# A decode layer's weight stream in five 32 KB load slots instead of ten of 16 KB

## The chip, the cores and the metric

The kernel runs on one core of one Trainium2 chip. The metric is the device time of one execution in microseconds, and lower is better. Before the change the median of three runs is 140.44 us (140.40 to 140.49).

## The reference

The kernel computes one decoding step of a transformer layer for four sequences of one token each: attention over the last 2048 entries of a KV cache, then a gated feed-forward block. All inputs are bfloat16.

```python
# x (4,1,1024); k_cache, v_cache (4,4,8192,128); wq (1024,4096); wo (4096,1024)
# w1, w3 (1024,3584); w2 (3584,1024);  W = 2048, 32 query heads on 4 KV heads, Dh = 128
q = (layernorm(x) @ wq) per head
p = softmax(q @ k[last W].T * Dh**-0.5)
h = x + (p @ v[last W]) @ wo
n = layernorm(h)
out = h + (silu(n @ w1) * (n @ w3)) @ w2
```

Four rows of activations meet 55.6 MB of caches and weights, and each of those bytes is read once.

## The kernel before

**The stream.** Everything large passes through a pool of `NSLOT = 10` slots of `SLOT = 8192` bfloat16 elements per partition, that is 16 KB on each of 128 partitions, 2 MB in all. `ring` is the order written out by hand: the keys of the four sequences, then the pieces of `wq` interleaved with four entries `kT` that take a slot but load nothing (they hold transposed keys), then values, `wo`, `w1`, `w3` and `w2`. An entry of k, v, `wq` and `wo` is 2 MB, one contiguous run of 16 KB on each partition. `w1` and `w3` come in four entries each of two weight rows, 14 KB on each partition. `w2` comes in blocks of 8, 8, 8, 2 and 2 rows (`W2B`), a row being 2 KB per partition. That is 29 loads, all issued by SyncE (SP) at L118.

**When a load is issued.** `fill` (L110) walks through the ring as long as the entry ten places before has been marked by `done`; the tile pool then makes SP wait until the last reader of the slot has finished. SP takes its loads in order. Completion is counted on eight semaphores used in turn, so that a load also waits until the load eight before it (counting the four small loads of x on ScalarE's queue) has landed.

**The stages on TensorE**, in the order in which they are written:

1. Keys are transposed (L226) in blocks of eight and copied to `kT` by VectorE (L228) and ScalarE (L230) in turn.
2. The query projection (L244) consumes `wq` entry by entry, 16 matmuls for each.
3. For each sequence: `scores` (L279), `row_max`, `softmax` (L319), `transpose_p` (L331) and `output` (L354), staggered over the sequences by the loop at L375.
4. The output projection with `wo` (L419), the residual and the second layernorm (L429 to L203).
5. `up_projection` (L443) with `w1`, 16 matmuls for each entry; its exponential, reciprocal and product on ScalarE and VectorE (L457 to L461); then `up_projection` with `w3`, the product `hg` (L465) and its transpose `hg_T` (L210).
6. The down projection (L476) through `w2`, four matmuls per row, then the sum with `h1` (L486) and four small stores.

Of the kernel before, what the change touches and what calls it, by code (L numbers as in the profile page):

```python
# [10 lines left out]
P = 128  # L11
# [3 lines left out]
BF16 = mybir.dt.bfloat16  # L15
FP32 = mybir.dt.float32

NSLOT = 10
SLOT = 8192
NEG = -1.0e30  # L20


@with_exitstack
def kernel(
# [20 lines left out]
    nc = tc.nc  # L45

    B, _, D = A_x.shape
    Hkv, Sk, Dh = A_k_cache.shape[1], A_k_cache.shape[2], A_k_cache.shape[3]
    NQ = A_wq.shape[1]
# [3 lines left out]
    F = B_w1.shape[1]  # L53
    KC = D // P
# [14 lines left out]
    wq_v = A_wq.rearrange("(p kc) n -> p kc n", kc=KC)  # L69
    T = REP  # L70
    L5 = 8
    JR = W // R
    JB = 8
    JM = 4
    wo_v = A_wo.rearrange("(g p t) n -> p g (t n)", g=Hkv, t=T)
    w1_v = B_w1.rearrange("(p kc) f -> p kc f", kc=KC)
    w3_v = B_w3.rearrange("(p kc) f -> p kc f", kc=KC)
    w2_v = B_w2.rearrange("(p fc) n -> p fc n", fc=FC)
# [4 lines left out]
    ptpool = ctx.enter_context(tc.tile_pool(name="ptpool", bufs=3))  # L83
    stream = ctx.enter_context(tc.tile_pool(name="stream", bufs=NSLOT))
    ps = ctx.enter_context(tc.tile_pool(name="ps", bufs=1, space=bass.MemoryType.PSUM))
# [3 lines left out]
    def of_cache(cache, b):  # L89
        return cache[b, :, Sk - W : Sk, :].rearrange("g (i j) d -> i g (j d)", j=JR)  # L90

    ks = [("k", b, [JR, Dh], of_cache(A_k_cache, b)) for b in range(B)]
    vs = [("v", b, [JR, Dh], of_cache(A_v_cache, b)) for b in range(B)]
    kts = [("kT", b, [JR, P], None) for b in range(B)]
    wqs = [("wq", i, [2, NQ], wq_v[:, 2 * i : 2 * i + 2, :]) for i in range(KC // 2)]
    wos = [("wo", g, [1, T * D], wo_v[:, g : g + 1, :]) for g in range(Hkv)]
    ring = ks + [x for two in zip(kts, wqs) for x in two] + vs + wos
    for name, w_v in (("w1", w1_v), ("w3", w3_v)):
        for i in range(KC // 2):
            ring.append((name, i, [2, F], w_v[:, 2 * i : 2 * i + 2, :]))  # L100
    W2B = [8, 8, 8, 2, 2]
    f0 = 0
    for i, n in enumerate(W2B):
        ring.append(("w2", i, [n, D], w2_v[:, f0 : f0 + n, :]))
        f0 += n
    place = {(name, i): at for at, (name, i, _, _) in enumerate(ring)}
    views = []
    used = set()

    def fill():  # L110

        while len(views) < len(ring) and (len(views) < NSLOT or len(views) - NSLOT in used):
            name, i, shape, src = ring[len(views)]
            slot = stream.tile([P, SLOT], BF16, tag="slot", name="s_" + name)
            dst = slot[:, : int(np.prod(shape))]
            view = dst.rearrange("p (a b) -> p a b", a=shape[0])
            if src is not None:
                nc.sync.dma_start(out=dst if name in ("k", "v") else view, in_=src)  # L118
            views.append(view)

    def get(name, i):
        return views[place[(name, i)]]

    def done(name, i):
        used.add(place[(name, i)])
        fill()

    ctx.enter_context(tc.manual_schedule())
# [4 lines left out]
    for c in range(C):  # L133
        nc.scalar.dma_start(out=x_nat[R * c : R * c + B, :], in_=x_flat[:, c * DQ : (c + 1) * DQ])
    fill()

    ident = const.tile([P, P], BF16)
# [8 lines left out]
        out=t32[:], in_=ident[:].rearrange("p (q h) -> p h q", q=C), axis=AX.X, op=ALU.add  # L146
# [4 lines left out]
    for q in range(C):  # L151
# [3 lines left out]
        out=negm[:], in_=t32[:].rearrange("p (g r) -> p g r", g=Hkv), axis=AX.X, op=ALU.add  # L155
    )
    nc.vector.tensor_scalar(
        out=negm[:], in0=negm[:], scalar1=-1.0, scalar2=-NEG, op0=ALU.add, op1=ALU.mult
    )
    jmask = const.tile([P, JM, 1], FP32)  # L160
    nc.vector.tensor_reduce(
        out=jmask[:, :, 0], in_=ident[:].rearrange("p (j h) -> p j h", j=JM), axis=AX.X, op=ALU.add
# [6 lines left out]
    for l in range(2):  # L169
        nc.gpsimd.tensor_copy(  # L170
            out=strip[:, l, B - 1 :].rearrange("p (c x) -> p c x", c=C)[:, :, : B * Hkv].rearrange(
                "p c (g b) -> p c g b", b=B
            )[:, :, :, 0],
            in_=t32[:].rearrange("p (g c l) -> p l c g", g=Hkv, c=C)[:, l],
# [45 lines left out]
    for b in range(B):  # L220
        k = get("k", b)
        kT = get("kT", b)
        for jb in range(JR // JB):
            kt_ps = ps.tile([P, JB, P], BF16, tag=f"kt{n_step % 3}")
            for jj in range(JB):
                nc.tensor.transpose(out=kt_ps[:, jj], in_=k[:, jb * JB + jj, :], identity=ident[:])  # L226
            if n_step % 2 == 0:
                nc.vector.tensor_copy(out=kT[:, jb * JB : (jb + 1) * JB], in_=kt_ps[:])  # L228
            else:
                nc.scalar.copy(out=kT[:, jb * JB : (jb + 1) * JB], in_=kt_ps[:])  # L230
            n_step += 1
        done("k", b)
# [1 line left out]

    q_ps = [ps.tile([P, REP // 2, Dh], FP32, tag=f"sc{hf}", name=f"q_ps{hf}") for hf in range(2)]
    HALF = REP // 2
    for i in range(KC // 2):
        w = get("wq", i)
        for kk in range(2):
            kc = 2 * i + kk  # L240
            for hf in range(2):
                for c in range(C):
                    o = (2 * c + hf) * HALF * Dh
                    nc.tensor.matmul(  # L244
                        q_ps[hf][R * c : R * c + R],
                        lhsT=xn_T[:, kc, :],
                        rhs=w[:, kk, o : o + HALF * Dh],
                        start=(kc == 0),
                        stop=(kc == KC - 1),
                        tile_position=(0, R * c),  # L250
                    )
        done("wq", i)
# [10 lines left out]
    for b in range(B):  # L263
        nc.vector.tensor_copy(  # L264
            out=Qm[:, b].rearrange("p (g y) -> p g y", y=QW)[:, :, :REP],
            in_=qT_ps[:, :, :, b].rearrange("p r g -> p g r"),
# [8 lines left out]
    def scores(b, gs):  # L275
        v = get("kT", b).rearrange("p j (q i g) -> p g q j i", q=C, g=Hkv)
        for g in gs:
            for q in range(C):
                nc.tensor.matmul(  # L279
                    sc_ps[b][R * q : R * q + R],  # L280
                    lhsT=Qm[:, b, g * R : (g + 1) * R],
                    rhs=v[:, g, q],
                    start=(g == 0),
                    stop=(g == Hkv - 1),
                    tile_position=(0, R * q),
                )
        if Hkv - 1 in gs:
            done("kT", b)
# [103 lines left out]
    for l in range(2):  # L392
# [15 lines left out]
        out=oP[:, :, :, :B],  # L408
        in_=oX[:, :, : Hkv * B].rearrange("p t (g b) -> p g t b", b=B),
# [4 lines left out]
    for g in range(Hkv):  # L414
        w = get("wo", g)
        for t in range(T):
            for c in range(C):
                o = t * D + c * DQ
# [14 lines left out]


    def up_projection(name, out_ps):
        for i in range(KC // 2):
            w = get(name, i)
            for kk in range(2):
                kc = 2 * i + kk
                for hf in range(2):  # L440
                    for c in range(C):
                        o = c * FQ + hf * FH
                        nc.tensor.matmul(  # L443
                            out_ps[hf][R * c : R * c + R],
                            lhsT=hn_T[:, kc, :],
                            rhs=w[:, kk, o : o + FH],
                            start=(kc == 0),
                            stop=(kc == KC - 1),
                            tile_position=(0, R * c),
                        )  # L450
            done(name, i)

    gu_ps = [ps.tile([P, FH], FP32, tag=f"sc{i}", name=f"gu_ps{i}") for i in range(4)]
    up_projection("w1", gu_ps[:2])
    eg = act.tile([P, 2, FH], FP32)
    for hf in range(2):
# [3 lines left out]
    for hf in range(2):  # L460
        nc.vector.tensor_tensor(out=eg[:, hf], in0=gu_ps[hf][:], in1=eg[:, hf], op=ALU.mult)  # L461
    up_projection("w3", gu_ps[2:])
    hg = act.tile([P, 2, FH], BF16)
    for hf in range(2):
# [6 lines left out]
    fc = 0  # L471
    for i, n in enumerate(W2B):
        w = get("w2", i)
# [46 lines left out]
```

## Time and profile before

| | |
|---|---|
| median of 3 runs | 140.44 us |
| the profiled execution's own time | 140.35 us |
| its span, first to last instruction | 138.5 us |
| outside the span | 1.85 us |
| read from HBM | 55.58 MB, mean 401 GB/s over the span |
| TensorE matmul / VectorE / ScalarE / GpSimd busy | 76.9 / 52.5 / 43.2 / 4.2 us |
| mean granted TensorE clock | 0.787 of full speed |

The page gives busy time by engine, the span in 40 slices with the DMA engines' busy share and rate, the traffic of each DMA queue, and the chain of work that ended last. Besides the page, the answers of the trace used below are the table by stretches of time, the timeline of single engines, and the records of DMA packets. A packet record is one descriptor on one of the 16 DMA engines: its queue, size, start and duration; a packet of 4 bytes is the mark with which one engine reports that its part of a load has landed.

### The profile page before, as it was taken

Reading aid. Unit: us, or ns where it says so; the run is one execution under the profiler, and the core shown is the slowest. Engines: PE = TensorE matmul, PEld = TensorE weight load, DVE = VectorE, ACT = ScalarE, POOL = GpSimd, SP = SyncE. Lnnn points to the kernel's source line nnn. Section 1 sums busy time; section 2 is a strip of 40 time slices with the busy share of each in tenths; the row PEclk is TensorE's granted clock in tenths of the full one; section 3 lists DMA queues with packets and bytes.
Section 4 is the critical chain, followed back from the end, with each engine's and each line's share of the span. In section 5 each row is a group of like instructions: output and inputs, shape, how many; then the busy total and the mean of one; then the engine's idle time right before and its main releaser. Section 6 shows DMA issues by size and latency. Waiting matters only on the chain.

```text
span 138.5 us, 2042 instructions
## 1 busy us (share of the span) xinstructions
PE 76.9 (55%) x868; PEld 45.8 (33%) x868; DVE 52.5 (38%) x97; ACT 43.2 (31%) x57; POOL 4.2 (3%) x18
## 2 busy tenths in 40 slices
PE   0009999971153799059639979483632432352280
PEld 0009988851011332024223535372311110142150
DVE  3026566630000334457365595515249700610001
ACT  2103799970000508999419600000420000000000
POOL 7400000000000000000000000000000000000000
PEclk9999999999555559955995999999999555555555
DMA  4999999999999999999999999999999999999940
GB/s 147 403 432 445 426 416 440 421 421 435 426 421 440 421 428 426 416 435 435 416 435 433 416 440 410 435 414 435 418 431 426 426 427 431 421 435 431 390 182 2
DMA packets 4249, 55.72 MB, mean 402 GB/s; under 512 B 496, under 2 KB 528, under 8 KB 784
## 3 DMA queue, kind: packets, MB, share of 16 engines
q1 hardware_dynamic: 4192, 55.58, 94.8%
q8 instruction: 7, 0.11, 0.3%
q10 hardware_dynamic: 48, 0.01, 0.0%
q14 instruction: 2, 0.02, 0.0%
HBM read 55.58 MB, written 0.01 MB: 401 GB/s over the span
## 4 chain that ended last, share of the span: by engine, by line
DMA 68%; PE 18%; DVE 6%; ACT 4%; issue 1%; SPq 1%; DVEq 0%
DMA s_w<-in_B_w_dram 38%; DMA s_wq<-in_A_wq_dram 24%; PE o_ps L354 10%; DMA s_k<-in_A_k_cache_dram 6%; ACT P L319 4%; PE sc_ps L279 4%; DVE PT L331 2%; PE q_ps L244 1%; PE nm_ps L308 1%; SPq L118 1%; DVE rmax L293 1%; PE mx_ps L295 1%; PE qT_ps L258 1%; DVE om L371 1%; PE tot_ps L340 1%
## 5 line engine op out<-in xcount | busy, mean ns | idle before, releaser
L319 ACT ACTIVATE P<-sc_ps,bias 128x512 bf16<-128x512 f32 x16 | 19.7, 1420 | 9.9 <-DVE bias L316 9.9
L226 PE MATMUL kt_ps<-ident,s_k 128*128 128x128 bf16 x256 | 18.4, 232 | 0.3
L226 PEld LDWEIGHTS <-s_k 128*128 128x128 bf16 x256 | 16.8, 105 | 1.9 <-issue 1.2
L354 PE MATMUL o_ps<-s_v,PT 128*128 128x512 bf16 x64 | 17.5, 435 | 0.0
L230 ACT COPY s_kT<-kt_ps 128x1024 bf16<-128x1024 bf16 x16 | 16.2, 1012 | 2.2 <-PE kt_ps L226 1.3
L443 PE MATMUL gu_ps<-s_w,n_T 128*32 128x448 bf16 x128 | 9.2, 435 | 13.4 <-DMA s_w<-in_B_w_dram 11.6
L228 DVE COPY s_kT<-kt_ps 128x1024 bf16<-128x1024 bf16 x16 | 11.1, 691 | 6.0 <-PE kt_ps L226 6.0
L476 PE MATMUL y_ps<-s_w,hg_T 128*32 128x256 bf16 x112 | 6.7, 416 | 9.4 <-DMA s_w<-in_B_w_dram 9.4
L244 PE MATMUL q_ps<-s_wq,n_T 128*32 128x512 bf16 x64 | 5.9, 503 | 10.4 <-DMA s_wq<-in_A_wq_dram 10.4
L331 DVE STREAM_TRANSPOSE PT<-P 128x2048 bf16<-128x2048 bf16 x4 | 9.2, 2302 | 2.7 <-ACT P L319 2.7
L354 PEld LDWEIGHTS <-PT 128*128 128x128 bf16 x64 | 7.1, 116 | 8.9 <-issue 4.2
L443 PEld LDWEIGHTS <-n_T 128*32 128x32 bf16 x128 | 3.9, 109 | 18.0 <-issue 14.6
L279 PE MATMUL sc_ps<-s_kT,Qm 128*32 128x512 bf16 x64 | 8.8, 608 | 0.4 <-DVE Qm L264 0.4
L193 ACT ACTIVATE rstd<-rstd,eps_t 128x4 f32<-128x4 f32 x2 | 0.6, 298 | 26.7 <-DVE rstd L192 26.7
L476 PEld LDWEIGHTS <-hg_T 128*32 128x32 bf16 x112 | 4.7, 138 | 11.7 <-issue 7.6
L183 PE MATMUL sums_ps<-both,ones_f 128*128 128x64 f32 x4 | 1.1, 374 | 11.9 <-DVE both L181 11.9
L254 DVE CAST q_sb<-q_ps 128x512 bf16<-128x512 f32 x1 | 0.7, 692 | 15.5 <-PE q_ps L244 15.5
L244 PEld LDWEIGHTS <-n_T 128*32 128x32 bf16 x64 | 2.0, 112 | 13.4 <-issue 12.7
L363 DVE SCALAR_TENSOR_TENSOR od<-o_ps,rinv,jmask 128x512 f32<-128x512 f32 x4 | 3.0, 750 | 8.0 <-PE o_ps L354 7.9
L295 PE MATMUL mx_ps<-ident_f,rmax 128*1 128x128 f32 x8 | 1.9, 333 | 7.4 <-DVE rmax L293 7.4
L459 DVE RECIPROCAL eg<-eg 128x896 f32<-128x896 f32 x1 | 5.8, 5754 | 0.0
L486 DVE TENSOR_TENSOR res<-y_ps,h 128x256 bf16<-128x256 f32 x1 | 0.4, 425 | 13.6 <-PE y_ps L476 13.6
(68 smaller groups left out, 62.4 us busy)
## 6 DMA issues: line engine op xcount, KB each, us to landing
s_w<-in_B_w_dram SPq DMA_DIRECT2D x8, 1792.0 KB, 25.4
s_k<-in_A_k_cache_dram SPq DMA_DIRECT2D x4, 2048.0 KB, 14.0
s_wq<-in_A_wq_dram SPq DMA_DIRECT2D x4, 2048.0 KB, 20.5
s_v<-in_A_v_cache_dram SPq DMA_DIRECT2D x4, 2048.0 KB, 27.9
s_wo<-in_A_wo_dram SPq DMA_DIRECT2D x4, 2048.0 KB, 27.4
s_w<-in_B_w_dram SPq DMA_DIRECT2D x3, 2048.0 KB, 32.7
s_w<-in_B_w_dram SPq DMA_DIRECT2D x2, 512.0 KB, 31.6
x_nat<-in_A_x_dram ACTq DMA_DIRECT2D x4, 2.0 KB
```

The lines of the kernel that those rows point to most:

```text
L226: nc.tensor.transpose(out=kt_ps[:, jj], in_=k[:, jb * JB + jj, :], identity=ident[:])
L228: nc.vector.tensor_copy(out=kT[:, jb * JB : (jb + 1) * JB], in_=kt_ps[:])
L230: nc.scalar.copy(out=kT[:, jb * JB : (jb + 1) * JB], in_=kt_ps[:])
L244: nc.tensor.matmul(q_ps[hf][R * c : R * c + R], lhsT=xn_T[:, kc, :], rhs=w[:, kk, o : o + HALF * Dh], start=(kc == 0), stop=(kc == KC - 1) ...
L279: nc.tensor.matmul(sc_ps[b][R * q : R * q + R], lhsT=Qm[:, b, g * R : (g + 1) * R], rhs=v[:, g, q], start=(g == 0), stop=(g == Hkv - 1), t ...
L295: nc.tensor.matmul(mx_ps[:1, :], lhsT=rmax[:], rhs=ident_f[:], start=True, stop=True)
L319: nc.scalar.activation(out=P4[:, :, :, g], in_=sc_ps[b][:].rearrange("p (j i) -> p j i", i=L5), func=ACT.Exp, bias=bias[:, g : g + 1], sca ...
L331: nc.vector.transpose(out=PT[:].rearrange("p j h -> p (j h)"), in_=stage.pop(("P4", b))[:].rearrange("p j i g -> p (j i g)"),)
L354: nc.tensor.matmul(o_ps[:], lhsT=PT[:, i * JM : (i + 1) * JM, :].rearrange("p j h -> p (j h)"), rhs=v[:, i * JM : (i + 1) * JM, :], start= ...
L443: nc.tensor.matmul(out_ps[hf][R * c : R * c + R], lhsT=hn_T[:, kc, :], rhs=w[:, kk, o : o + FH], start=(kc == 0), stop=(kc == KC - 1), til ...
L459: nc.vector.reciprocal(out=eg[:], in_=eg[:])
L476: nc.tensor.matmul(y2_ps[R * c : R * c + R, :], lhsT=hg_T[:, fc, :], rhs=w[:, ff, c * DQ : (c + 1) * DQ], start=(fc == 0), stop=(fc == FC ...
```

## The change

The ten slots of 16 KB per partition become five of 32 KB. A slot now holds a list of parts:

- k, v, `kT` and `wo` are put in pairs, two entries of 16 KB in one slot, each still loaded by its own DMA.
- `wq`, `w1` and `w3` come in entries of four weight rows instead of two: one DMA with a contiguous run of 32 KB (`wq`) or 28 KB (`w1`, `w3`) on each partition. The loops over them take 32 matmuls per entry instead of 16.
- `w2` is cut into 1, 15, 8, 2 and 2 rows. The 15 rows are one DMA with 30 KB per partition. The first row is loaded in five DMAs over the partitions 0-111, 112-119, 120-123, 124-125 and 126-127.
- `wq`'s first entry moves ahead of the `kT` entries.

A slot is filled again once all of its parts are used. The matmuls are the same, in the same order.

```diff
-NSLOT = 10
-SLOT = 8192
+NSLOT = 5
+SLOT = 16384
+PIECES = [0, 112, 120, 124, 126, 128]
...
-    wqs = [("wq", i, [2, NQ], wq_v[:, 2 * i : 2 * i + 2, :]) for i in range(KC // 2)]
-    ring = ks + [x for two in zip(kts, wqs) for x in two] + vs + wos
-    for name, w_v in (("w1", w1_v), ("w3", w3_v)):
-        for i in range(KC // 2):
-            ring.append((name, i, [2, F], w_v[:, 2 * i : 2 * i + 2, :]))
-    W2B = [8, 8, 8, 2, 2]
+    def pair(parts):
+        return [parts[0:2], parts[2:4]]
...
+    def four_rows(name, view, n):
+        return [[(name, i, [4, n], view[:, 4 * i : 4 * i + 4, :])] for i in range(KC // 4)]
+    wq_ = four_rows("wq", wq_v, NQ)
+    ring = k_ + wq_[:1] + kT_ + wq_[1:] + v_ + wo_ + four_rows("w1", w1_v, F) + four_rows("w3", w3_v, F)
+    W2B = [1, 15, 8, 2, 2]
...
+    ring += [w2_[:2], w2_[2:]]
...
     def fill():
-        while len(views) < len(ring) and (len(views) < NSLOT or len(views) - NSLOT in used):
...
+        while len(taken) < len(ring):
+            n = len(taken) - NSLOT
+            if n >= 0 and not all((name, i) in used for name, i, _, _ in ring[n]):
+                break
+            parts = ring[len(taken)]
+            slot = stream.tile([P, SLOT], BF16, tag="slot", name="s_" + parts[0][0])
+            o = 0
+            for name, i, shape, src in parts:
+                dst = slot[:, o : o + int(np.prod(shape))]
+                o += int(np.prod(shape))
+                view = dst.rearrange("p (a b) -> p a b", a=shape[0])
+                if (name, i) == ("w2", 0):
+                    for p0, p1 in zip(PIECES[:-1], PIECES[1:]):
+                        nc.sync.dma_start(out=view[p0:p1], in_=src[p0:p1])
+                elif src is not None:
+                    nc.sync.dma_start(out=dst if name in ("k", "v") else view, in_=src)
+                views[(name, i)] = view
+            taken.append(slot)
...
-    for i in range(KC // 2):
+    for i in range(KC // 4):
         w = get("wq", i)
-        for kk in range(2):
-            kc = 2 * i + kk
+        for kk in range(4):
+            kc = 4 * i + kk
```

`up_projection` is changed in the same way as the query projection.

More of the change, by code (lines that the diff above doesn't have):

```diff
@@ L90, in of_cache @@
         return cache[b, :, Sk - W : Sk, :].rearrange("g (i j) d -> i g (j d)", j=JR)
-    ks = [("k", b, [JR, Dh], of_cache(A_k_cache, b)) for b in range(B)]
-    vs = [("v", b, [JR, Dh], of_cache(A_v_cache, b)) for b in range(B)]
-    kts = [("kT", b, [JR, P], None) for b in range(B)]
-    wqs = [("wq", i, [2, NQ], wq_v[:, 2 * i : 2 * i + 2, :]) for i in range(KC // 2)]
-    wos = [("wo", g, [1, T * D], wo_v[:, g : g + 1, :]) for g in range(Hkv)]
-    ring = ks + [x for two in zip(kts, wqs) for x in two] + vs + wos
@@ L98 @@
-    for name, w_v in (("w1", w1_v), ("w3", w3_v)):
-        for i in range(KC // 2):
-            ring.append((name, i, [2, F], w_v[:, 2 * i : 2 * i + 2, :]))
-    W2B = [8, 8, 8, 2, 2]
+    def pair(parts):
+        return [parts[0:2], parts[2:4]]
+    k_, v_ = (
+        pair([(name, b, [JR, Dh], of_cache(cache, b)) for b in range(B)])
+        for name, cache in (("k", A_k_cache), ("v", A_v_cache))
+    )
+    kT_ = pair([("kT", b, [JR, P], None) for b in range(B)])
+    wo_ = pair([("wo", g, [1, T * D], wo_v[:, g : g + 1, :]) for g in range(Hkv)])
@@ L102 @@
+    def four_rows(name, view, n):
[3 more added lines that the diff above has]
+    W2B = [1, 15, 8, 2, 2]
+    w2_ = []
     f0 = 0
     for i, n in enumerate(W2B):
-        ring.append(("w2", i, [n, D], w2_v[:, f0 : f0 + n, :]))
+        w2_.append(("w2", i, [n, D], w2_v[:, f0 : f0 + n, :]))
         f0 += n
-    place = {(name, i): at for at, (name, i, _, _) in enumerate(ring)}
@@ L107 @@
-    views = []
+    ring += [w2_[:2], w2_[2:]]
+    views = {}
+    taken = []
     used = set()
     def fill():
-        while len(views) < len(ring) and (len(views) < NSLOT or len(views) - NSLOT in used):
[L113 to L119, printed above, removed]
+        while len(taken) < len(ring):
[16 more added lines that the diff above has]
+            taken.append(slot)
@@ L121, in get @@
     def get(name, i):
-        return views[place[(name, i)]]
+        return views[(name, i)]
     def done(name, i):
-        used.add(place[(name, i)])
+        used.add((name, i))
         fill()
@@ L435, in up_projection @@
     def up_projection(name, out_ps):
-        for i in range(KC // 2):
+        for i in range(KC // 4):
             w = get(name, i)
-            for kk in range(2):
-                kc = 2 * i + kk
+            for kk in range(4):
+                kc = 4 * i + kk
                 for hf in range(2):
```

## Prediction

> **What bounds the kernel.** I read the page first: busy time, the slices, the queues, the chain.
>
> ```profile
> PE 76.9 (55%) x868; PEld 45.8 (33%) x868; DVE 52.5 (38%) x97; ACT 43.2 (31%) x57; POOL 4.2 (3%) x18
> DMA  4999999999999999999999999999999999999940
> GB/s 147 403 432 445 426 416 440 421 421 435 426 421 440 421 428 426 416 435 435 416 435 433 416 440 410 435 414 435 418 431 426 426 427 431 421 435 431 390 182 2
> q1 hardware_dynamic: 4192, 55.58, 94.8%
> q8 instruction: 7, 0.11, 0.3%
> DMA 68%; PE 18%; DVE 6%; ACT 4%; issue 1%; SPq 1%; DVEq 0%
> ```
>
> No compute engine passes 55%. The DMA engines are full from the second slice to the 38th, at 416 to 440 GB/s whatever is loaded. SP's queue (q1) alone takes 94.8% of 16 engines' time. The stream is the bound, so only three things can move the end: time per byte, gaps between loads, and what follows the last landing.
>
> The timeline of TensorE shows the stream's beat, since the engine waits for every late load, and the stretches show its end.
>
> ```profile
> 33.96 1.05 PE L244 MATMUL q_ps<-s_wq,n_T 128*32 128x512 bf16 x16 [3.52 <-DMA s_wq<-in_A_wq_dram]
> 38.85 1.90 PE L244 MATMUL q_ps<-s_wq,n_T 128*32 128x512 bf16 x16 [3.85 <-DMA s_wq<-in_A_wq_dram]
> 43.75 1.90 PE L244 MATMUL q_ps<-s_wq,n_T 128*32 128x512 bf16 x16 [3.01 <-DMA s_wq<-in_A_wq_dram]
> 108.76 1.68 PE L443 MATMUL gu_ps<-s_w,n_T 128*32 128x448 bf16 x16 [3.36 <-DMA s_w<-in_B_w_dram]
> 113.06 1.69 PE L443 MATMUL gu_ps<-s_w,n_T 128*32 128x448 bf16 x16 [2.62 <-DMA s_w<-in_B_w_dram]
> 127.22 1.90 PE L476 MATMUL y_ps<-s_w,hg_T 128*32 128x256 bf16 x32 [3.00 <-DMA s_w<-in_B_w_dram]
> 132.12 2.33 PE L476 MATMUL y_ps<-s_w,hg_T 128*32 128x256 bf16 x40 [3.00 <-DMA s_w<-in_B_w_dram]
> 134.61 0.62 PE L476 MATMUL y_ps<-s_w,hg_T 128*32 128x256 bf16 x8 [0.17 <-DMA s_w<-in_B_w_dram]
> ```
>
> A load of 16 KB per partition lands every 4.89 us (38.85 - 33.96), one of 14 KB every 4.30 (113.06 - 108.76).
>
> ```profile
> 120.00:128.00 8.00, 2.68 (x48) 2.13 (x52) 1.67 (x1) 0.00 (x0) 0.00 (x0) 0.50 1.02 432
> 128.00:132.00 4.00, 1.12 (x24) 0.68 (x13) 0.00 (x0) 0.00 (x0) 0.00 (x0) 0.50 0.96 398
> 132.00:134.60 2.60, 2.33 (x40) 1.76 (x40) 0.00 (x0) 0.00 (x0) 0.00 (x0) 0.50 0.45 175
> ```
>
> The last three columns are clock, DMA share and GB/s. From 132.0 the DMA engines are only 45% busy: half have finished, half are late. The packet records say why. Eight engines report the last load between 132.57 and 132.90, eight between 133.15 and 134.16. Each late one was interrupted once, by one of six instruction fetches (16 KB, 0.96 to 1.11 us) or two 8 KB table loads; after a fetch the engine's next 16 KB packet took 1.10 to 1.16 us instead of 0.61. The fetch at 21.5 us put its engine's report about 1.5 us behind the others. **The end is set by the slowest late engine**, at 134.16; TensorE starts on the last two rows at 134.61, and the last instruction ends at 138.5.
>
> **The change, part by part.**
>
> *Fewer, longer descriptors.* Each engine serves eight partitions of every 128-partition load. `wq` goes from 32 descriptors per engine to 16, `w1` and `w3` from 64 to 32: 48 fewer. (`w2` has 40 before and about 40 after.) What does one cost beyond its bytes? On an undisturbed engine the reports of successive loads are 4.890 us apart (8 x 16 KB), 4.290 (8 x 14 KB) and 1.267 (8 x 4 KB); a report packet takes 9 ns. The first two give 0.600 us per 16,384 bytes, leaving 4.890 - 8 x 0.600 - 0.009 = 0.081 for eight descriptors: 10 ns each. The 4 KB beat by the same slope leaves 1.267 - 1.200 - 0.009 = 0.058: 7 ns each. I take 9, nearer to the long rows: 48 x 9 ns = 0.43 us (0.34 to 0.48). No row above 16 KB exists. If 28 to 32 KB rows were cut into packets of 14 to 16 KB, the saving is nil, and that is the lower bound; a slower stream is the third rival.
>
> [...]
>
> *Fewer reports, and `w2`'s first row.* A four-partition transfer leaves four 4-byte packets here (q10's 48 packets are six such transfers with four data and four report packets each), so a transfer uses only as many engines as divide its rows. The five pieces then use 16, 8, 4, 2 and 2 engines. If the small ones always use the lowest-numbered, engines 0 and 1 get 11 rows instead of 8, 2 and 3 get 9, 4 to 7 stay at 8, and 8 to 15 get 7. A 2 KB row is 0.075 us plus 0.009. Reports fall from 29 to 27 on engines 0 and 1, to 25, 24, and to 23 on the upper eight. Sums: engines 0-1 gain 0.43 + 0.02 - 0.25 = **0.20**; 2-3 gain 0.43 + 0.04 - 0.08 = **0.39**; 4-7 gain 0.43 + 0.05 = **0.48**; 8-15 gain 0.43 + 0.05 + 0.08 = **0.56**. The on-time engines have over a microsecond to spare, so the answer is the gain of the engine that is late. I can't see its number in the trace; I take 0.48, the middle, with 0.20 to 0.56 as ends.
>
> [...]
>
> *Issue.* SP issues 27 loads instead of 29, at 0.33 to 0.6 us each. The pieces are issued near 96 us, when the queue holds work until about 114. Free.
>
> *Coarser slots: does the queue run dry?* By the pool's allocation, v0 waits for the last key transposes (29.5 us, not 20.9; queue full until 41); `wo`'s first pair for all query matmuls (47 against 61); `w1`'s first half for the last scores (61.85 + 1.9 = 64 against 80); its second for sequence 1's output (77.87 + 1.9 = 80 against 88); `w3`'s halves for the last output and for `wo`'s first pair (88 against 97, 95 against 105); `w2` for the rest of `wo` and for landings (96 against 114). The least margin is 8 us. Free; without cover each microsecond late would be one at the end.
>
> *Later compute.* TensorE starts `wq`'s second half when all of it has landed: 16 matmuls more at 1.90 us, so attention shifts by about 1.9 us. The gate product, done at 110.1, moves to 112, and is needed after `w3`'s matmuls at 118.8. `w3` then has 32 matmuls after its last landing near 117: until 120.5, plus 1.16 and 1.70 on VectorE: `hg_T` at 123.7. `w2`'s 15 rows land near 126.3 (12 rows, 7.43 us, before the end), take 60 x 59 ns = 3.6 us, until 130; the next block lands near 131.6. Slack 1.6 us, so nothing reaches the end. The last four rows and the tail of 3.9 us stay.
>
> **Sum:** 140.35 - 0.48 = 139.87 for the profiled execution, which is 0.09 below the median of the runs: 139.96 us.
>
> **The rivals.**
>
> 1. *The late engine is 0 or 1.* Gain 0.20 to 0.30: about 140.2. For: eight of sixteen are late. Against: it must also be the slowest of them, which spread over a microsecond (133.15 to 134.16). 12%.
> 2. *No descriptor saving.* Rows are cut, or the restart after a fetch grows with the packet: the restart cost 0.55 us on 16 KB and 0.46 to 0.50 on 14 KB. If it went with size it would be about 0.95 on 28 KB, 0.45 more, eating the saving. Against: first packets into an idle engine also took 0.92 to 1.15 us, which looks like a latency. 140.35 to 140.5. 14%.
> 3. *Slower: long runs stream slower per byte.* They carry 27 of 55.6 MB, some 64 us. From 0.75% slower (0.48 / 64) the gain is gone; at 1.5% the time is 140.44 + 0.48 = 140.9. For: nothing so long was run. Against: 14 and 16 KB rows differ only by the fixed part. 14%.
> 4. *Faster: the clock.* `w2`'s rows run at half clock. A burst of 3.4 to 3.6 us is new; one at 47.4 to 52.1 us raised the clock to full at 52.1. At full clock the last eight matmuls would take about 0.2 us less: 139.75. It must fit the clock's windows and last through the 1.6 us pause. 8%.
>
> **How the numbers follow.** The forecast holds 52%: 139.96. With rival 4, faster by over 0.2% (0.28 us, about what can be told from no change) is 60%; rivals 1 and 2 make 26% within; rival 3 14% slower. The range 139.55 to 140.75 goes from the largest sum with the clock (140.44 - 0.56 - 0.2 = 139.68, and 0.13 for unknowns) through rivals 1 and 2 to the first part of rival 3.
>
> **What would show it.** Right: q1 packets down by about 800; `wq` rows as 32 KB packets near 1.21 us and 28 KB near 1.06; beats of 9.69 and 8.49 us instead of 9.78 and 8.58; DMA slices still 9; the last `w2` wait ending near 134.1; no wait of the DMA queue for `gu_ps` or `o_ps` that leaves the slices short. Wrong: 14 to 16 KB packets for those rows (rival 2), a beat above 9.78 (rival 3), a slice of 7 or 8 in midstream (a dry queue), restarts well above 0.55 us.

## The result and the profile after

The changed kernel takes 140.95 us (median of 7 runs, 140.74 to 141.19), the kernel before 140.48 (7 runs in all). The ratio is 1.0037 with a 95% interval of 1.0028 to 1.0046: slower by 0.4%, where 0.3% faster was forecast. The profiled execution took 141.06 us, 139.3 of them span.

The page of the changed kernel, with the lines that answer to those shown of before (busy time, slices, queue, chain):

```profile
PE 81.2 (58%) x868; PEld 48.1 (35%) x868; DVE 52.5 (38%) x97; ACT 42.7 (31%) x57; POOL 4.2 (3%) x18
DMA  4999999999989999999999999999999999999940
GB/s 151 410 420 447 438 400 442 452 447 452 452 362 424 419 438 433 409 428 442 414 431 438 426 439 436 449 420 412 461 408 428 412 412 325 424 424 400 399 180 2
q1 hardware_dynamic: 3344, 55.58, 94.7%
DMA 56%; PE 26%; DVE 11%; ACT 4%; issue 1%; SPq 0%; DVEq 0%
```

The stream is still the bound, with 848 packets fewer for the same bytes. Two slices are low. The one with 362 GB/s, near 40 us, is a matter of counting: with 32 KB packets a slice of 3.5 us holds one round of packets more or less, and with the packets spread over their durations it has 431 GB/s. The one with 325, near 117 us, is real (298 GB/s when spread), although its busy share is still 9: the packets there became longer, not fewer.

The timeline of TensorE in the changed kernel, at the same waits as those shown of the kernel before:

```profile
33.91 3.60 PE L264 MATMUL q_ps<-s_wq,n_T 128*32 128x512 bf16 x32 [4.42 <-DMA s_wq<-in_A_wq_dram]
43.63 3.60 PE L264 MATMUL q_ps<-s_wq,n_T 128*32 128x512 bf16 x32 [6.12 <-DMA s_wq<-in_A_wq_dram]
117.86 3.18 PE L463 MATMUL gu_ps<-s_w,n_T 128*32 128x448 bf16 x32 [7.73 <-DMA s_w<-in_B_w_dram]
127.83 3.39 PE L496 MATMUL y_ps<-s_w,hg_T 128*32 128x256 bf16 x60 [3.88 <-DMA s_w<-in_B_w_dram]
132.72 1.06 PE L496 MATMUL y_ps<-s_w,hg_T 128*32 128x256 bf16 x32 [1.50 <-DMA s_w<-in_B_w_dram]
133.99 0.40 PE L496 MATMUL y_ps<-s_w,hg_T 128*32 128x256 bf16 x8 [0.21 <-DMA s_w<-in_B_w_dram]
135.28 0.62 PE L496 MATMUL y_ps<-s_w,hg_T 128*32 128x256 bf16 x8 [0.89 <-DMA s_w<-in_B_w_dram]
```

The last two rows of `w2` start at 135.28 instead of 134.61. The 15 rows start at 127.83; before, the 16th row started with its block at 127.22, so the changed kernel was already 0.6 late by then.

The reports of the loads (the 4-byte packets) put the loss between two loads. The first engine to report `w3`'s last rows does so at 114.62 us, against 115.09 before: 0.47 early. The first to report the 16th row of `w2` does so at 125.62, against 124.88: 0.74 late. **1.2 us were lost while `w2`'s first row passed.** The table by stretches shows it; the last columns are granted clock, DMA share and GB/s. First the kernel before, then the changed one:

```profile
114.00:117.00 3.00, 0.75 (x8) 0.15 (x1) 0.00 (x0) 0.00 (x0) 0.00 (x0) 0.50 1.03 436
117.00:119.00 2.00, 1.57 (x16) 0.49 (x15) 0.21 (x1) 0.00 (x0) 0.00 (x0) 0.50 1.02 434
```

```profile
114.00:117.00 3.00, 0.00 (x0) 0.00 (x0) 2.82 (x3) 0.00 (x0) 0.00 (x0) 0.57 0.91 276
117.00:119.00 2.00, 1.14 (x16) 0.56 (x19) 0.00 (x0) 0.00 (x0) 0.00 (x0) 0.50 1.21 410
```

276 instead of 436 GB/s for 3 us is 1.1 us of work left over, 410 instead of 434 for 2 us another 0.1. The table counts a packet whole in the stretch in which it starts; with packets spread over their durations both stretches are slow, at 329 and 314 GB/s against 427 and 429, and the loss is the same 1.2 us. The packet records show that it is not the small packets alone: 28 KB packets of `w3` on engines that had not yet reached the first row took up to 1.72 us instead of 1.06, and the first 30 KB packets up to 1.80 instead of 1.14. From 119 us on they are 1.14 again. So the packets of several engines were slow at the same time, for some 3.7 us; what slowed them is in no record.

### The profile page after: what moved, and what is told of

It is laid out like the page before. It is cut to its first block, busy times and chain, and to the rows that moved or that the text cites. A ratio compares the mean times of both kernels' runs of the same rounds, so it can differ in the third digit from the quotient of the medians.

```text
span 139.3 us, 2029 instructions
## 1 busy us (share of the span) xinstructions
PE 81.2 (58%) x868; PEld 48.1 (35%) x868; DVE 52.5 (38%) x97; ACT 42.7 (31%) x57; POOL 4.2 (3%) x18
## 4 chain that ended last, share of the span: by engine, by line
DMA 56%; PE 26%; DVE 11%; ACT 4%; issue 1%; SPq 0%; DVEq 0%
DMA s_w<-in_B_w_dram 26%; DMA s_wq<-in_A_wq_dram 25%; PE o_ps L374 11%; DMA s_k<-in_A_k_cache_dram 5%; PE y_ps L439 4%; ACT P L339 4%; PE sc_ps L299 4%; DVE PT L351 3%; PE q_ps L264 2%; DVE om L391 2%; DVE od L383 2%; PE tot_ps L360 1%; PE nm_ps L328 1%; PE on_ps L414 1%; DVE rmax L313 1%
## 5 line engine op out<-in xcount | busy, mean ns | idle before, releaser
L374 PE MATMUL o_ps<-s_v,PT 128*128 128x512 bf16 x64 | 19.4, 473 | 0.0
L246 PEld LDWEIGHTS <-s_k 128*128 128x128 bf16 x256 | 17.4, 107 | 1.8 <-issue 1.7
L250 ACT COPY s_kT<-kt_ps 128x1024 bf16<-128x1024 bf16 x16 | 15.7, 1012 | 3.1 <-PE kt_ps L246 3.1
L463 PE MATMUL gu_ps<-s_w,n_T 128*32 128x448 bf16 x128 | 9.8, 474 | 9.6 <-DMA s_w<-in_B_w_dram 7.7
L264 PE MATMUL q_ps<-s_wq,n_T 128*32 128x512 bf16 x64 | 7.2, 629 | 10.5 <-DMA s_wq<-in_A_wq_dram 10.5
L374 PEld LDWEIGHTS <-PT 128*128 128x128 bf16 x64 | 7.7, 126 | 10.4 <-issue 6.7
L496 PE MATMUL y_ps<-s_w,hg_T 128*32 128x256 bf16 x112 | 5.8, 361 | 9.1 <-DMA s_w<-in_B_w_dram 6.5
L463 PEld LDWEIGHTS <-n_T 128*32 128x32 bf16 x128 | 4.4, 122 | 14.3 <-issue 11.3
L496 PEld LDWEIGHTS <-hg_T 128*32 128x32 bf16 x112 | 3.9, 122 | 11.3 <-issue 7.4
L264 PEld LDWEIGHTS <-n_T 128*32 128x32 bf16 x64 | 2.7, 138 | 14.3 <-issue 14.2
L439 PE MATMUL y_ps<-s_wo,oP 128*32 128x256 bf16 x128 | 5.0, 333 | 1.5 <-DVE oP L427 1.5
```

The costliest lines, as they stand in the source:

```text
L264: nc.tensor.matmul(q_ps[hf][R * c : R * c + R], lhsT=xn_T[:, kc, :], rhs=w[:, kk, o : o + HALF * Dh], start=(kc == 0), stop=(kc == KC - 1) ...
L374: nc.tensor.matmul(o_ps[:], lhsT=PT[:, i * JM : (i + 1) * JM, :].rearrange("p j h -> p (j h)"), rhs=v[:, i * JM : (i + 1) * JM, :], start= ...
L439: nc.tensor.matmul(y_ps[R * c : R * c + R, :], lhsT=oP[:, g, t, :], rhs=w[:, 0, o : o + DQ], start=(g == 0 and t == 0), stop=(g == Hkv - 1 ...
L463: nc.tensor.matmul(out_ps[hf][R * c : R * c + R], lhsT=hn_T[:, kc, :], rhs=w[:, kk, o : o + FH], start=(kc == 0), stop=(kc == KC - 1), til ...
L496: nc.tensor.matmul(y2_ps[R * c : R * c + R, :], lhsT=hg_T[:, fc, :], rhs=w[:, ff, c * DQ : (c + 1) * DQ], start=(fc == 0), stop=(fc == FC ...
```

## The experiments

Unless a ratio is given, times are medians of 4 to 11 runs. The kernel before, run beside each group of experiments, took 140.31 to 140.47 us. A figure "over e1" is a difference of two medians, often from different groups, between which the kernel before itself varied by 0.16 us.

### The pieces or the long rows

Run e1 loads the first row whole, e2 in two pieces, e3 together with the next 15:

```diff
-PIECES = [0, 112, 120, 124, 126, 128]
+PIECES = [0, 128]          # e1 and e3
+PIECES = [0, 112, 128]     # e2
...
-    W2B = [1, 15, 8, 2, 2]
+    W2B = [16, 8, 2, 2]    # e3
...
-    ring += [w2_[:2], w2_[2:]]
+    ring += [w2_[:1], w2_[1:]]    # e3
```

> The changed kernel with w2's first row as one load over 128 partitions. In the changed kernel the 28 KB rows of w3's second half were all reported 0.47 us earlier than in the kernel before, and the 16th row of w2 0.74 us later: 1.2 us were lost between the two. Theory A (the five pieces cost it): the loss goes, about 140.95 - 1.2 = 139.75 us, and the 30 KB packets take 1.14 us from the first on. Theory B (30 KB rows that start one row into w2's partition line, or the step from w3 to w2 with long rows, stall the engines): unchanged, about 140.9, with first 30 KB packets near 1.7 us.

> The changed kernel with w2's first row in two pieces, partitions 0-111 and 112-127: every engine carries eight rows again, none of the transfers with 8, 4, 2 and 2 partitions is left, but seven partitions per engine stay. Theory A1 (the small transfers on few engines cost it): about 139.8 us. Theory A2 (a split that gives an engine other partitions than the 128-partition loads do costs it): 140.5 to 141. Theory B: 140.9.

> The changed kernel with w2 in blocks of 16, 8, 2 and 2 rows, the first row with the others in one load of 32 KB per partition. Theory A (pieces): about 139.7 us, a little under the run with one piece, since eight descriptors of 2 KB per engine go. Theory B in the form 'long rows of w2 stall': about 140.9; in the form 'a start one row into the line': 139.7 as well, and then the run with one piece stays at 140.9 and tells the two apart.

Run e4 puts the five pieces into the kernel before:

```diff
+PIECES = [0, 112, 120, 124, 126, 128]
...
-    W2B = [8, 8, 8, 2, 2]
+    W2B = [1, 7, 8, 8, 2, 2]
...
-            if src is not None:
+            if (name, i) == ("w2", 0):
+                for p0, p1 in zip(PIECES[:-1], PIECES[1:]):
+                    nc.sync.dma_start(out=view[p0:p1], in_=src[p0:p1])
+            elif src is not None:
```

> The kernel before with w2 in blocks of 1, 7, 8, 8, 2 and 2 rows and the first row in the five pieces, all else as it was. Theory A: about 140.45 + 1.2 = 141.6 us, with packets of 14 to 16 KB slowed near 116 to 119 us. Theory B, or a cost that pieces have only beside long rows: 140.4 to 140.6.

| run | us | ratio to before, 95% interval |
|---|---|---|
| e1, one piece | 139.72 | 0.9955 (0.9942 to 0.9967) |
| e2, 112 and 16 | 140.83 | 1.0029 (1.0017 to 1.0040) |
| e3, 16 rows in one load | 139.86 | 0.9958 (0.9945 to 0.9970) |
| e4, before with the pieces | 141.63 | 1.0080 (1.0066 to 1.0094) |

The five pieces cost 1.23 us in the changed kernel (140.95 - 139.72) and 1.16 in the kernel before (141.63 - 140.47), whatever the length of the rows around them. In e4 it is 14 KB packets of `w3` that stretch, to 0.6 to 0.95 us instead of 0.54 between 115.3 and 118.8 us. Two pieces of 112 and 16 partitions, without the loads of 8, 4, 2 and 2, cost nearly as much, 1.11 us. Long rows and `w2`'s start one row into the line cost nothing. The same two stretches of e1:

```profile
114.00:117.00 3.00, 0.11 (x4) 0.11 (x7) 0.63 (x2) 0.00 (x0) 0.00 (x0) 0.50 1.07 447
117.00:119.00 2.00, 2.00 (x24) 0.95 (x25) 0.00 (x0) 0.00 (x0) 0.00 (x0) 0.50 0.93 399
```

Full rate again; the mean of the five microseconds is 428 GB/s, and the last rows start 1.19 us earlier than in the changed kernel:

```profile
134.09 0.62 PE L496 MATMUL y_ps<-s_w,hg_T 128*32 128x256 bf16 x8 [0.67 <-DMA s_w<-in_B_w_dram]
```

### Which splits, and how much of them

```diff
-PIECES = [0, 112, 120, 124, 126, 128]
+PIECES = [0, 64, 128]      # e5
+PIECES = [0, 96, 128]      # e7
+PIECES = [0, 112, 128]     # e6, and
...
-                if (name, i) == ("w2", 0):
+                if (name, i) == ("w2", 1):     # e6: the block of 15 rows
```

> The changed kernel with w2's first row in two pieces of 64 partitions: four partitions per engine and piece, eight rows per engine in all. Theory C (any split that does not give an engine the partitions it has in the 128-partition loads jams the stream): about 140.8 us, as with pieces of 112 and 16, and again 28 to 30 KB packets of 1.5 us and more. Theory D (only counts that don't fall on whole groups of partitions, seven per engine, do it): 139.7 to 139.9.

> The changed kernel with w2's first row in pieces of 96 and 32 partitions (six and two per engine). Theory C and theory D both: about 140.8 us. If it is near 139.8 the seven of the 112-partition piece is special.

> The changed kernel with w2's first row as one load and the block of 15 rows in two pieces of 112 and 16 partitions: fifteen times the bytes in the split form. Theory C1 (the stream loses a share of its rate for as long as split loads run; in the changed kernel about a third over 3.7 us): the 15 rows take 9 us undisturbed, so some 4 to 5 us are lost, about 144 us. Theory C2 (a fixed cost of stepping into and out of a split load): about 140.8 us. If each split byte costs what it did for one row, 1.1 us for 0.26 MB, it is about 156 us.

Run e8 has the row whole and the small loads once more into free space:

```diff
-PIECES = [0, 112, 120, 124, 126, 128]
+PIECES = [112, 120, 124, 126, 128]
...
-    W2B = [1, 15, 8, 2, 2]
+    W2B = [1, 14, 9, 2, 2]
...
                 if (name, i) == ("w2", 0):
+                    nc.sync.dma_start(out=view, in_=src)
+                    spare = slot[:, 15 * D :].rearrange("p (a b) -> p a b", a=1)
                     for p0, p1 in zip(PIECES[:-1], PIECES[1:]):
-                        nc.sync.dma_start(out=view[p0:p1], in_=src[p0:p1])
+                        nc.sync.dma_start(out=spare[p0:p1], in_=src[p0:p1])
```

> The changed kernel with w2 in 1, 14, 9, 2 and 2 rows, the first row as one load over 128 partitions, and after it the small loads of partitions 112-119, 120-123, 124-125 and 126-127 once more into a free part of the same slot, where nothing reads them: the small transfers on few engines alone, without the split of 112. They add at most four rows of 2 KB to engines 0 and 1, 0.33 us, on engines that may not be the late ones. If the small transfers have a part in the 1.23 us: 140.0 to 140.9. If the 112-partition split does it all: 139.7 to 140.0.

| run | us (all its runs) | over e1 |
|---|---|---|
| e5, halves | 141.25 (140.92 to 141.49) | 1.53 |
| e7, 96 and 32 | 140.92 (140.76 to 141.01) | 1.20 |
| e6, 15 rows as 112 and 16 | 150.42 (149.30 to 152.35) | 10.70 |
| e8, small loads beside the whole row | 140.29 (140.21 to 140.45) | 0.57 |

Every split costs. Halves seem to cost most, but the single runs of e5 and e7 overlap. The 15 rows cost 10.7 us (10.0 without the slowest of the four runs). That is at least twice the 4 to 5 us that I expected from a rate of two thirds, and less than the some 16 us at the cost per byte of the single row. The slices of e6:

```profile
GB/s 145 427 435 443 421 509 426 421 417 421 421 408 421 426 417 421 448 426 428 426 432 452 399 450 422 438 427 422 445 415 446 239 255 263 227 111 123 416 234 2
```

At first the stream runs at 227 to 263 GB/s, then at 111 and 123. In these last two slices it is not that engines have finished: by the packet records all sixteen are busy until 138 us. The second piece, one 30 KB packet on each engine into partitions 112 to 127, takes up to 4.30 us a packet instead of 1.14 (3.95 to 4.30 on the last eight), and the 16 KB packets of the plain load behind it take 1.9 to 2.5 us instead of 0.61 until 136 us. With packets spread over their durations, the stream moves 244 to 312 GB/s under the piece of 112 partitions and 124 to 148 under the piece of 16. The small loads by themselves cost up to 0.57 us, but added to the split of 112 only 0.12 (140.95 against 140.83, within the spread of the runs), so the two costs do not add up; this run also cuts `w2` differently.

The loss could arise where a split load is written or where it is read. Run e12 has the dose of e6 in halves; run e9 leaves the load whole and deals out its source rows:

```diff
+PIECES = [0, 64, 128]      # e12, for ("w2", 1) as in e6
...
+                    nc.sync.dma_start(      # e9, for ("w2", 1)
+                        out=dst, in_=src.rearrange("(i q) a n -> q i (a n)", q=16)
+                    )
```

> The changed kernel with w2's first row as one load and the block of 15 rows in two pieces of 64 partitions. From the run with pieces of 112 and 16 for the same rows (10.7 us over the run with one piece) and from the first row alone (1.53 us lost with halves, 1.20 with 96 and 32, 1.11 with 112 and 16): if the loss goes with the crowding of the split, 10 to 15 us, 150 to 155 us. If the loss is a stall at the step between unlike loads, about 141. [...]

> The changed kernel with w2's first row as one load, and the block of 15 rows as one load over 128 partitions whose source rows are dealt out in another order: of the first sixteenth of the partitions the source rows are 0, 16, 32 and so on, so each engine reads other places of HBM than it usually does, while the destinations are those of a 128-partition load. (The 15 rows of w2 then meet other rows of h, so that part of the sum is another one; the work is the same.) Theory W (the split loads jam where SBUF is written): about 139.8 us, as with one piece. Theory R (they jam where HBM is read): near the 150.4 us of the 15 rows in pieces of 112 and 16, in any case over 142.

e12 took 151.64 us, 11.9 over e1; its 30 KB packets have a median of 2.38 us against 1.14. e9 took 151.32, which looked like a jam on the reading side. But its source has 16 outer rows, and that may also change how the destination is cut into sixteen. Three more runs separated the two:

```diff
-  in_=src.rearrange("(i q) a n -> q i (a n)", q=16)
+  in_=src.rearrange("(i q) a n -> q i (a n)", q=32)                               # e13
+  ap=[[8 * row, 16], [row + D, 8], [1, 15 * D]]     # e14, over the same tensor
+  ap=[[4 * row, 32], [row + D, 4], [1, 15 * D]]     # e15
```

> As the run with the spread source, but dealt out by 32 instead of 16: the source is 32 outer by 4 inner rows, the form in which the key loads come, which land at the full beat of 4.89 us. [...] (These rows of w2 again meet other rows of h.) Theory R (the reading of spread rows jams): 145 us or more. Theory W (the writing jams, and only when the cut gives an engine another set of partitions than the plain loads do; a source of 16 outer rows forces such a cut, one of 32 does not): 139.7 to 140.0 us.

> As the run with one piece, but the 15-row load's source is written as 16 outer by 8 inner rows, each inner row starting 2 KB later in its line than the one before (so part of the sum uses other elements of w2): engine by engine the source lies where a run of eight partitions has it. Theory W: the cut into runs of eight consecutive partitions jams, about 150 us. Theory R: nothing is spread, 139.7 to 140.0 us.

> The same with 32 outer by 4 inner rows, again each inner row 2 KB later in its line. Theory W: 139.7 to 140.0 us, in contrast to 16 by 8. Theory R: 139.7 to 140.0 as well. If it is near 150, the odd source rows themselves are slow and the pair says nothing on W.

| source of the 15-row load | 32 outer rows | 16 outer rows |
|---|---|---|
| spread over all 128 lines of `w2` | 139.81 (e13) | 151.32 (e9) |
| near its usual place | 139.83 (e15) | 150.99 (e14) |

Where the source lies makes no difference; the number of outer rows makes all of it. (In these four runs `w2`'s rows meet other rows of `h` than in the layer; the bytes and the work are the same.) The slices of e14, then of e15:

```profile
GB/s 145 436 427 430 430 470 452 426 422 430 422 395 422 426 426 422 426 439 433 430 422 460 407 458 400 454 407 443 415 446 437 206 189 231 214 179 199 413 246 2
```

```profile
GB/s 153 410 428 437 423 432 451 456 451 428 399 404 428 428 423 432 423 423 442 423 416 432 439 445 449 395 441 432 437 407 449 432 437 415 428 428 404 387 188 2
```

From the 32nd slice e14 runs at 179 to 231 GB/s, half of 430, with 30 KB packets of 2.37 us (median); e15 shows nothing. So where in HBM the bytes lie does not make the jam. What is left is how the load is cut among the engines, and I take it to be which partitions an engine writes. Another cut would also change which source rows an engine reads, so that a jam on the reading side which goes with the cut alone is not excluded by these four runs. A trace has no addresses, so no run shows which rows an engine reads and which partitions it writes; that 16 outer rows make another cut than 32, as theory W has it, is my inference.

The packets go with the times: against 1.14 us, the median in the changed kernel, the 30 KB packets are 2.1 times as long in e12 (2.38) and in e14 (2.37), up to 3.8 times (4.30) in the second piece of e6, and not longer in e13 and e15. Why one form is slower than another is not shown.

### The slots alone

Run e10 keeps the five slots and gives all loads the sizes they had before:

```diff
-    W2B = [1, 15, 8, 2, 2]
+    W2B = [8, 8, 8, 2, 2]
...
-                if (name, i) == ("w2", 0):
-                    for p0, p1 in zip(PIECES[:-1], PIECES[1:]):
-                        nc.sync.dma_start(out=view[p0:p1], in_=src[p0:p1])
+                if name in ("wq", "w1", "w3"):
+                    for a in (0, 2):
+                        nc.sync.dma_start(out=view[:, a : a + 2], in_=src[:, a : a + 2])
```

> The five 32 KB slots of the changed kernel with all loads of the size they had before: wq, w1 and w3 in two loads of 14 or 16 KB per partition for each slot, w2 in 8, 8, 8, 2 and 2 rows. If the gain of the run with one piece (0.75 us) is that of longer descriptors, this is the kernel before: 140.2 to 140.6 us. If the slots or the order bring or cost something by themselves, it differs from 140.4 by more than 0.3.

140.36 us, ratio 1.0001 (0.9992 to 1.0010): the coarser slots, the new order and the later release of slots cost and bring nothing. The gain of e1 over the kernel before is that of the longer descriptors, with the other cut of `w2` in it.

## Why the prediction was wrong

**Right: the bound and the descriptors.** The stream bounds both kernels. The rows came as packets of 32 KB (1.213 us) and 28 KB (1.065). From the first report of the first keys to that of `w3`'s last rows the changed kernel needs 107.14 us, the kernel before 107.59: 0.45 us less. Up to there the forecast's terms make 0.48: 48 x 9 ns = 0.43 for descriptors and 0.05 for six reports fewer. The other runs repeat it: 107.10 to 107.23 us with the long rows, 107.55 and 107.62 in e4 and e10 with the short ones. The beat of a 32 KB load is 9.68 us on an engine without interruption. The restart after an instruction fetch did not grow with the packet, as rival 2 feared: a 28 KB packet then took 1.52 or 1.53 us, a 32 KB packet 1.71, which is 0.46 to 0.50 more than usual. (The two 8 KB packets called table loads in the prediction stand on the profile's page as instruction, q14, like the 16 KB ones of q8.) So rivals 2 (no saving) and 3 (long runs stream slower) are out, although rival 3 had the right sign and nearly the right time; the mechanism was another. Over the whole run e1 gains 0.63 us by the ratio and 0.75 by the medians. The rest beyond 0.45 is about what the first reports vary between runs (7.28 to 7.53 us) and is not explained further.

**Wrong: "Fewer reports, and `w2`'s first row".** This step priced the five pieces by rows and reports on each engine: between 0.23 us lost and 0.13 gained beside the descriptors, 0.05 gained in the middle. Measured, they cost 1.23 us. The step counted how many bytes an engine gets; it left out that the whole stream was slow while the split ran (276 GB/s against 436 from 114 to 117 us). The counts themselves came true: 392 reports in all are what 16, 8, 4, 2 and 2 engines for the five pieces give. Why a split is slow is open: that it goes with which partitions an engine writes fits the times, but no run shows those partitions. With the measured cost the forecast's sum is 139.96 + 1.23 = 141.19; e1, the run without the pieces, was 0.24 below 139.96, and so the changed kernel is at 140.95. The range ended 0.2 short of it. Every large load of the trace before spans 128 partitions; for a split one there was no row at all, and the bound had to be open on the side of a loss.

**Rival 1** (the late engine is 0 or 1) could not be told: what it would shift, 0.2 us, is below the jam.

**Free, as predicted: issue and dry queue.** e10 shows it for the slots. The pieces were issued from 99.6 to 101.3 us, later than the 96 I gave, and still waited in the queue until 114.6. **Later compute** stayed hidden, but with less room than I worked out. This is VectorE at the gate product, first before (L461), then in the changed kernel (L481), and at the product's use (L485):

```profile
108.92 1.16 DVE L461 TENSOR_TENSOR eg<-gu_ps,eg 128x448 f32<-128x448 f32 x2
115.77 1.16 DVE L481 TENSOR_TENSOR eg<-gu_ps,eg 128x448 f32<-128x448 f32 x2
120.71 1.16 DVE L485 TENSOR_TENSOR hg<-gu_ps,eg 128x448 bf16<-128x448 f32 x2 [3.79 <-PE gu_ps L463]
```

The product is ready at 116.93, not at 112: the query projection ran 1.7 us longer after its last landing, near the 1.9 forecast; I did not foresee that later matmuls would meet the half clock more often (the 64 of `o_ps` took 19.4 us instead of 17.5, the 128 of `wo` 5.0 instead of 3.7; the granted clock was 0.56 instead of 0.73 in the first 16 of `o_ps` and 0.72 instead of 1.00 in those of `wo`). The wait ahead of L485 is still for `w3`'s matmuls, and `hg_T` was ready at 123.60; the forecast's 123.7 is 0.3 above its own terms (120.5 + 1.16 + 1.70). Another reading was loose: the slices given as 416 to 440 GB/s run from 390 to 445. Nothing in the sum rests on either.

**Rival 4** happened in part: the granted clock, which in both traces keeps a value for 3.41 us or a multiple of it, was 1.00 from 131.49 to 134.91 us, and so for the block after the 15 rows (32 matmuls in 1.06 us). For the last eight, from 135.28, it was 0.50, and they took 0.62 us as before.

## What to carry to other kernels

Load all 128 partitions at once, and write the source of such a load with 32 or 128 outer rows (139.72 to 139.83 us here) rather than 16 (150.99 and 151.32). A split by partitions, even of one row of 2 KB per partition in a 55 MB stream, slowed the plain loads beside it too (28 KB packets of up to 1.72 us instead of 1.06). If a load must be uneven, try it in a busy stream before pricing it by how many bytes each engine gets; here that price was 0.05 us gained, and 1.23 us were lost. Longer contiguous rows were worth it in this stream, which never stops: 48 descriptors fewer per engine brought 0.45 us, and e1, the change without the pieces, beats both kernels at 139.72 us.

## What was not expected of the hardware

- The jam reached engines that did not run split rows: `w3`'s 28 KB packets, in plain loads, stretched from 1.06 to 1.72 us.
- A load over all 128 partitions ran at half rate too (179 to 231 GB/s) when only its source was written as 16 outer rows instead of 32 (150.99 against 139.83 us).
- The cost per split row was not constant: 1.1 us for one row of 256 KB, 0.7 for each of 15 (10.7 / 15).
- The 15 rows in halves lose 11.9 us. Twice their undisturbed 9.1 us would lose 9.1. The rest is in the trace: the low rate lasts some 22 us, from 116 to 138, because the engines finish their split rows between 133.4 and 138.1 us, and until then the plain 16 KB packets behind them are slow too (mostly 1.2 to 1.3 us instead of 0.61, up to 136.5). Why the engines end so far apart is open.
- A narrow piece was slower still: 16 partitions of 30 KB took up to 4.30 us a packet (e6) instead of 1.14.
